# Attention scores of four heads on 32 rows each with three half-precision products, six score banks and half-bank projections

## The chip, the cores and the metric

The kernel runs on one core of one Trainium2 chip. The metric is the device time of one execution in microseconds (us); the time of a kernel is the median of several runs. The core has TensorE (PE, matrix multiplication into PSUM), VectorE (DVE), ScalarE (ACT), GpSimd (POOL) and SyncE (SP, here the queue that issues most transfers). PSUM has eight banks, each of 512 single-precision columns on 128 partitions.

## The reference

The input is one sequence of 2048 positions with 1024 features. Two layers follow each other, and each has an attention block and a spectral block (a two-dimensional Fourier filter). The change is in the attention block.

```python
def _A_ref(x, wqkv, wo):
    B, S, D = x.shape                      # 1, 2048, 1024
    H = 32
    Dh = D // H                            # 32
    qkv = (x @ wqkv).reshape(B, S, 3, H, Dh).transpose(2, 0, 3, 1, 4)
    q, k, v = qkv[0], qkv[1], qkv[2]
    scores = jnp.einsum("bhqd,bhkd->bhqk", q, k) * (Dh ** -0.5)
    p = _softmax(scores, axis=-1)
    o = jnp.einsum("bhqk,bhkd->bhqd", p, v)
    return o.transpose(0, 2, 1, 3).reshape(B, S, D) @ wo

x = A_x
x = x + _A_ref(_layernorm(x), A_wqkv, A_wo)
x = x + _B_ref(_layernorm(x), B_w_r, B_w_i)
x = x + _A_ref(_layernorm(x), A_wqkv, A_wo)
x = x + _B_ref(_layernorm(x), B_w_r, B_w_i)
```

## The kernel before

The 32 heads are worked in eight groups `g` of four heads. A group has four chunks `c` of 512 queries and sixteen key tiles `kt` of 128 keys. Everything is transposed: the features lie on partitions, and a score tile has keys on partitions and queries along the free dimension.

Projections work on values that `split` has cut into a high and a low float16 half (ScalarE writes the high half, L160, VectorE the rest, L161). `qk_chunk` makes 512 positions of the queries or keys of a group: eight feature blocks by three products (high by high, high by low, low by high) accumulate in one PSUM bank (L305), then `split` reads the bank into `hl`. `v_tile` does the same for 128 positions of the values of two groups, 256 columns wide (L372), and ScalarE alone reads the bank (L376).

The queries and keys of four heads come out one below the other, 32 features each. They are stored to a DRAM tile `db` (L315) and loaded again (`spread`, L329) so that each head's tile has four blocks of 32 rows: for the keys high, high, low, low, and for the queries high, low, high, low. One matmul over 128 rows therefore gives the sum of all four products of the halves for one head (`S`, L551). Two heads share a PSUM tile `s` of two banks, and ScalarE takes the exponential of the 1024 columns (L553) into `p`, in single precision. The bias of the exponential is a bound worked out from the norms of queries and keys (`norms`, `mkbias`).

`PV` (L561) multiplies `p` by the values: four heads, each 32 output columns, write the four quarters of the partitions of one bank `o`, over the sixteen key tiles. VectorE adds the tiles of `p` up (L564, L566) into `acc` for the denominators. After the last key tile `fin` sums `acc` over partitions with ones (L571, in an `x` bank), and VectorE transposes, inverts and multiplies (L573 to L579).

The order of instructions on TensorE is the order of the program. For each key tile it issues the scores of two heads, some steps of a filler, the scores of the other two heads, more of the filler. At even key tiles it issues the value matmuls of the two earlier key tiles. The filler is the projections of the groups to come, and in the last group and the end of the one before, the output projection (`wo_part` without the last group of heads, `wo_tile` with it, L438), whose result VectorE adds to the residual (L452, L466).

PSUM holds two score tiles of two banks each, two `o` banks, and two `x` banks that serve the projections, the norms, the denominators and the output projection in turn:

```python
    psS = psum("at_psS", 2, space=PSUM)
    psO = psum("at_psO", 2, space=PSUM)
    psX = psum("at_psX", 2, space=PSUM)
```

Of the kernel before, what the change touches and what calls it, by code (L numbers as in the profile page):

```python
# [100 lines left out]
SX = 2.0 ** 8  # L101
# [5 lines left out]
WO_STEPS = 12 * 48  # L107
# [74 lines left out]
class AttnPools:  # L182


    def __init__(self, tc):
        self.tc = tc
        self.low = Pools(tc, "left")
        self.big = self.low("at_x", 1).tile([128, 16384], F32, name="big")
        self.right = Pools(tc, "right")
        r = self.right("at_r", 1).tile([128, 16384], F32, name="R")  # L190
        self.x = r.rearrange("p (t d) -> p t d", d=1024)
        k = r.bitcast(F16).rearrange("p (t h n) -> p t h n", h=4, n=2048)
        self.k = [k[:, i] for i in (1, 2)]
# [10 lines left out]
    def open_small(self):  # L204
        small = self.small = Pools(self.tc, "left")
        self.pp = small("at_p", 7)
        self.qp = small("at_q", 2)
        self.hl = small("at_hl", 2)
# [46 lines left out]
SPILL = [2, 3, 8, 9, 10, 11]  # L255
# [3 lines left out]
def attention(nc, tc, layer, ap, xin, yd, xnd, wts, wo, cst, dram, flags):  # L259
# [5 lines left out]
    pp, qp, hl, sgp, wqp, wvp = ap.pp, ap.qp, ap.hl, ap.sgp, ap.wqp, ap.wvp  # L265
    sq, on, on2, sm = ap.sq, ap.on, ap.on2, ap.sm
    db = psum("at_db", 20, space=DRAM)
# [5 lines left out]
    V, K, Q, kd, qd, bias, nrm, mx = {}, {}, {}, {}, {}, {}, {}, {}  # L273
    cur = [0]
# [24 lines left out]
    def qk_chunk(ph, c):  # L299
        kind, g = ph  # L300
        w = W[ph]
        ps = psX.tile([128, 512], F32, name="x")
        for d in range(8):
            for i, (a, b) in enumerate(((w[:, 0, d], xh[c][:, d]), (w[:, 0, d], xl[c][:, d]), (w[:, 1, d], xh[c][:, d]))):
                nc.tensor.matmul(ps, a, b, start=d == 0 and i == 0, stop=d == 7 and i == 2)  # L305
                if d < 7 or i < 2:
                    yield
        t = hl.tile([128, 2, 512], F16, name="hl")
        split(nc, t[:, 0], t[:, 1], ps, SQ / (SX * SW))
        if c == 0:  # L310
            p_, n_ = (qp, "Q") if ph == ("q", 0) else (sq, "sq")
            nrm[ph] = p_.tile([128, 4, 512], BF16, name="sq", tag=n_)
        nc.gpsimd.tensor_tensor(nrm[ph][:, c], t[:, 0], t[:, 0], op=ALU.mult)  # L313
        d_ = db.tile([2, 128, 512], F16, name="db")
        nc.sync.dma_start(d_.rearrange("a p n -> p a n"), t)  # L315
        if kind == "k":
            if c == 0:
                K[g] = ap.k[g % 2]
            kd[g, c] = d_
            if g <= cur[0] + 1:  # L320
                load_k(g)
        else:
            qd[g, c] = d_
        yield

    def spread(dst, d_, parts):

        for j, a in enumerate(parts):
            nc.sync.dma_start(dst[32 * j:32 * j + 32], d_[a].rearrange("(h p) n -> p h n", p=32))  # L329

    def load_k(g):
        for c in range(NCH):
            if (g, c) in kd:
                spread(K[g][:, :, c * 512:(c + 1) * 512], kd.pop((g, c)), (0, 0, 1, 1))

    def load_q(g, c):
        Q[g, c] = qp.tile([128, 4, 512], F16, name="Q")
        spread(Q[g, c], qd.pop((g, c)), (0, 1, 0, 1))

    def norms(ph):  # L340
        kind, g = ph
        if g not in mx:
            mx[g] = sm.tile([128, 2], F32, name="mqk")
        ps = psX.tile([128, 512], F32, name="x")
        for c in range(4):
            nc.tensor.matmul(ps[32 * c:32 * c + 32], cst["bones"], nrm[ph][:, c], start=True, stop=True)
        i = 0 if kind == "k" else 1
        nc.vector.reduce_max(mx[g][:, i:i + 1], ps, axis=AX.X)
        if kind == "q":
            mkbias(g)  # L350
        yield

    def mkbias(g):
        r = sm.tile([128, 2], F32, name="mall")
        nc.gpsimd.partition_all_reduce(r, mx[g], 128, bass.bass_isa.ReduceOp.max)
        b = sm.tile([128, 1], F32, name="bpr")
        nc.gpsimd.tensor_tensor(b, r[:, 0:1], r[:, 1:2], op=ALU.mult)
# [4 lines left out]
    def v_tile(ph, t):  # L362
# [5 lines left out]
        ps = psX.tile([128, 512], F32, name="x")  # L368
        for d in range(8):
            a, b = xh[c][:, d, o:o + 128], xl[c][:, d, o:o + 128]  # L370
            for i, (l, r) in enumerate(((a, w[:, 0, d]), (a, w[:, 1, d]), (b, w[:, 0, d]))):
                nc.tensor.matmul(ps[:, :256], l, r, start=d == 0 and i == 0, stop=d == 7 and i == 2)  # L372
                if (3 * d + i) % 2 and d * 3 + i < 23:
                    yield
# [12 lines left out]
    def filler():  # L387
        run(prep(phases[0]))
        for i, ph in enumerate(phases):
# [12 lines left out]
            for n, _ in enumerate(body()):  # L402
                if n % 16 == 12:
                    next(nxt, None)
                yield
# [23 lines left out]
    def wo_mm(c, t, n, ds):  # L429

        p = psX.tile([128, 512], F32, name="x")
        last = 3 * len(ds) - 1
        k = 0
        for d in ds:
            oh, ol = ((olast[c][:, i] if d == 7 else osb[c][:, i, d])[:, t * 128:t * 128 + 128] for i in range(2))
            wh, wl = (wo_t[i][d // 4][:, d % 4, n * 512:n * 512 + 512] for i in range(2))
            for a, b in ((oh, wh), (oh, wl), (ol, wh)):
                nc.tensor.matmul(p, a, b, start=k == 0, stop=k == last)  # L438
                k += 1
                if k <= last:  # L440
                    yield
        return p

    def wo_part(c, t, dst):
# [4 lines left out]
        for n in range(2):  # L449
            p = yield from wo_mm(c, t, n, range(7))  # L450
            sl = slice(n * 512, n * 512 + 512)
# [3 lines left out]
    def wo_tile(c, t, dst, part=False):  # L455
# [6 lines left out]
        for n in range(2):  # L462
            p = yield from wo_mm(c, t, n, (7,) if part else range(8))
            sl = slice(n * 512, n * 512 + 512)
            src = dst if part else x
            nc.vector.scalar_tensor_tensor(x[:, sl], p, 1.0 / (SO * SW), src[:, sl], op0=ALU.mult, op1=ALU.add)  # L466
            nc.vector.bn_stats(st[:, n], x[:, sl])
            if not part:
                fold(nc, x, dst, slice(4 * n, 4 * n + 4))
            if n:  # L470
# [8 lines left out]
    def wo_filler():  # L479
# [10 lines left out]
        while rests:  # L490
# [3 lines left out]
            elif parts and (parts[0] < 11 or pos[0] > 98):  # L494
# [4 lines left out]
                if t == 10:  # L499
                    dst[t] = sq.tile([128, 1024], F32, name="sq")  # L500
                if t == 11:
                    dst[t] = qp.tile([128, 1024], F32, name="Q")
# [3 lines left out]
            else:  # L506
                yield True
# [32 lines left out]
    load_q(0, 0)  # L540
# [6 lines left out]
    def S(g, c, kt, hf):  # L547
        s = psS.tile([128, 2, 512], F32, name="s")
        for j in range(2):
            h = hf * 2 + j  # L550
            nc.tensor.matmul(s[:, j], K[g][:, h, kt * 128:(kt + 1) * 128], Q[g, c][:, h], start=True, stop=True)  # L551
        p = P[g, c, kt, hf] = pp.tile([128, 2, 512], F32, name="p")
        nc.scalar.activation(p, s, AF.Exp, bias=bias[g], scale=SCALE / (SQ * SQ))  # L553

    def PV(g, c, kt, hf):
        if kt == 0 and hf == 0:
            O[g, c] = psO.tile([128, 512], F32, name="o")
        p = P[g, c, kt, hf]
        for j in range(2):
            h = hf * 2 + j  # L560
            nc.tensor.matmul(O[g, c][32 * h:32 * h + 32], V[g][:, kt, 32 * h:32 * h + 32], p[:, j],  # L561
                             start=kt == 0, stop=kt == NKT - 1)
        if kt == 1:
            nc.vector.scalar_tensor_tensor(acc[hf], P[g, c, 0, hf], 1e-34, p, op0=ALU.add, op1=ALU.add)  # L564
        elif kt:
            nc.vector.tensor_add(acc[hf], acc[hf], p)  # L566

    def fin(g, c):
        z = psX.tile([128, 512], F32, name="x")
        for h in range(4):  # L570
            nc.tensor.matmul(z[32 * h:32 * h + 32], cst["ones"], acc[h // 2][:, h % 2], start=True, stop=True)  # L571
        zt = on.tile([128, 16, 32], F32, name="zt")
        nc.vector.transpose(zt.rearrange("p a b -> p (a b)"), z)  # L573
# [14 lines left out]
    pend = []  # L588
    fill, lwo, wof = filler(), load_wo(), wo_filler()
    left, n_wo, go = 16, 0, 0  # L590
    with tc.manual_schedule(engines={mybir.EngineType.PE}):
        for g in range(NG):
            cur[0] = g
            total = sum(steps(ph) for ph in beside.get(g, []))
            got = 0
            for u in range(NCH * NKT):
                c, kt = divmod(u, NKT)
                for hf in range(2):
                    S(g, c, kt, hf)
                    i = 2 * u + hf + 1  # L600
                    pos[0] = i if g == NG - 1 else 0
                    if i == 4 and (g + 1, 0) in kd:
                        load_k(g + 1)
                    nq = (g, c + 1) if c + 1 < NCH else (g + 1, 0)
                    if i % 32 > 2 and nq in qd:
                        load_q(*nq)
                    while got < min(total, total * i / (126 if g < NG - 2 else 112)):
                        next(fill, None)
# [4 lines left out]
                    if g == NG - 1 or (g == NG - 2 and got == total and not left):  # L613
                        go += (WO_STEPS - n_wo) / (129 - i + 128 * (NG - 1 - g))
                        while n_wo + 1 <= go:
                            if next(wof, None):
# [3 lines left out]
                    pend.append((g, c, kt, hf))  # L620
                    while hf and kt % 2 == 0 and len(pend) > 2:
                        w = pend.pop(0)
                        PV(*w)
                        if w[2] == NKT - 1 and w[3] == 1:
                            fin(w[0], w[1])
            if (g + 1, 0) in qd:
                load_q(g + 1, 0)
            if g == NG - 2:
                run(lwo)
        for w in pend:  # L630
# [4 lines left out]
    for i, t, n in ((0, 2, 2), (2, 8, 4)):  # L635
# [19 lines left out]
def spectral(nc, tc, ap, yd, xout, a, cst, fast, flags=None, nxt=None):  # L655
# [221 lines left out]
    def ai(i, tt):  # L877
# [6 lines left out]
        if i % 2 == 0:  # L884
            sd[0] = ap.qp.tile([128, 8, 128], F32, name="sd0", tag="Q")
            sd[1] = ap.pp.tile([128, 8, 128], F32, name="sd1", tag="p")
# [247 lines left out]
```

## Time and profile before

| | |
|---|---|
| median of 3 runs | 4070.28 us (4067.77 to 4073.4) |
| the profiled execution | 4067.89 us, span of the core 4066.1 us, granted TensorE clock 0.99 |
| TensorE busy | 3883.5 us, 96% of the span |
| VectorE busy | 3279.8 us, 81% |
| ScalarE busy | 2823.8 us, 69% |
| GpSimd busy | 711.7 us, 18% |
| attention loop, layer 1 | first score matmul at 123.4 us |
| attention loops, end | last score matmul of layer 2 at 3745.0 us |

A line of a group in the page has the line of the kernel, the engine, the operation, what it writes and reads, shapes and count; behind the bar the busy time in us and the mean in ns of one instruction; behind the second bar the time in which the engine had been idle just before such an instruction, and what ended it. Matmuls are pipelined, so the mean of one (379 ns) is longer than the time by which it advances the engine. PEld is the loading of the weights, which overlaps matmuls. In a timeline the two first columns are the start and the time covered by the merged instructions, both in us.

### The profile page before, as it was taken

The page shows a single profiled execution, that of the slowest core. Times are in us where ns is not written, and L with a number is a line of the kernel's source. Part 1 is how long each engine was busy: PE and PEld are TensorE (multiplying, and loading weights), DVE is VectorE, ACT ScalarE, POOL GpSimd, SP SyncE. Part 2 cuts the span into 40 slices and gives each one's busy share as a digit, 9 for nine tenths or more (in the row PEclk, how much of TensorE's full clock was granted, in tenths as well). Part 3 has the DMA queues.
Part 4 walks back from the last instruction along what each step waited for, and adds up shares of the span by engine and source line. Part 5 has one row for each costly group of instructions (what it writes and reads, how often), then busy time and mean ns, then how long its engine had stood idle before and what let it go on. Part 6 is the DMA issues. An engine that isn't in the chain of part 4 may idle for free.

```text
span 4066.1 us, 65193 instructions
## 1 busy us (share of the span) xinstructions
PE 3883.5 (96%) x25012; PEld 1843.3 (45%) x25012; DVE 3279.8 (81%) x4059; ACT 2823.8 (69%) x3597; POOL 711.7 (18%) x625
## 2 busy tenths in 40 slices
PE   8899999999999999999888999999999999999998
PEld 5333533443344333378853335334433443333797
DVE  6698889889988988956755987888888889889456
ACT  4577777777777865548645777777777778655485
POOL 1111011101210112314311110111011101122143
PEclk9999999999999999999989999999999999999999
DMA  4221022102200323253132210221022003232433
GB/s 149 66 63 53 17 60 64 44 19 68 65 30 24 97 71 103 89 204 96 52 120 66 63 53 17 63 66 39 19 71 63 29 24 101 71 100 90 157 109 99
DMA packets 209378, 289.64 MB, mean 71 GB/s; under 512 B 17696, under 2 KB 161696, under 8 KB 208032
## 3 DMA queue, kind: packets, MB, share of 16 engines
q1 hardware_dynamic: 207312, 279.03, 21.5%
q10 hardware_dynamic: 1744, 6.36, 0.4%
q8 instruction: 198, 3.24, 0.3%
q14 instruction: 124, 1.02, 0.1%
HBM read 197.23 MB, written 88.08 MB: 70 GB/s over the span
## 4 chain that ended last, share of the span: by engine, by line
PE 74%; issue 8%; DVE 8%; ACT 4%; POOL 3%; DMA 2%; ACTq 0%; DVEq 0%; POOLq 0%; SPq 0%
PE o L561 20%; PE s L551 19%; PE x L305 13%; PE x L372 7%; PE x L438 5%; ACT p L553 3%; DVE R L566 2%; PE ps L767 2%; PE ps L705 1%; PE x L571 1%; DMA w<-in_w 1%; POOL sq L313 1%; PE ps L696 1%; PE ps L882 1%; PE ps L870 1%
## 5 line engine op out<-in xcount | busy, mean ns | idle before, releaser
L553 ACT ACTIVATE p<-s,bias 128x1024 f32<-128x1024 f32 x2048 | 2168.0, 1117 | 851.3 <-PE s L551 816.8
L566 DVE TENSOR_TENSOR R<-R,p 128x1024 f32<-128x1024 f32 x1792 | 2189.9, 1273 | 237.7 <-ACT p L553 233.0
L551 PE MATMUL s<-Q,R 128*128 128x512 f16 x4096 | 1219.9, 380 | 49.9 <-ACT p L553 47.9
L561 PE MATMUL o<-p,R 128*32 128x512 f32 x8192 | 991.4, 600 | 0.0
L305 PE MATMUL x<-big,wqk 128*128 128x512 f16 x3072 | 858.8, 379 | 2.3 <-DVE hl L161 2.3
L551 PEld LDWEIGHTS <-R 128*128 128x128 f16 x4096 | 357.4, 97 | 811.8 <-issue 559.0
L305 PEld LDWEIGHTS <-wqk 128*128 128x128 f16 x3072 | 299.9, 98 | 365.1 <-issue 6.8
L561 PEld LDWEIGHTS o<-p,R 128*32 128x32 f32 x8192 | 218.1, 109 | 513.0 <-issue 508.1
L372 PE MATMUL x<-wv,big 128*128 128x256 f16 x3072 | 425.5, 274 | 15.3 <-DVE hl L161 5.9
L313 POOL TENSOR_TENSOR sq<-hl 128x512 bf16<-128x512 f16 x128 | 200.5, 1567 | 1191.4 <-ACT hl L160 1191.0
L372 PEld LDWEIGHTS <-big 128*128 128x128 f16 x3072 | 300.7, 98 | 161.6 <-DVE big L161 6.8
L438 PE MATMUL x<-big 128*128 128x512 f16 x1344 | 334.8, 379 | 3.8 <-DVE xres L466 2.8
L582 POOL TENSOR_TENSOR ohl<-zt,ohl 128x512 f16<-128x512 f32 x64 | 102.6, 1602 | 1221.4 <-ACT ohl L581 1179.1
L438 PEld LDWEIGHTS <-big 128*128 128x128 f16 x1344 | 131.1, 98 | 164.7 <-issue 6.2
L564 DVE SCALAR_TENSOR_TENSOR R<-p 128x1024 f32<-128x1024 f32 x128 | 153.2, 1197 | 26.8 <-ACT p L553 26.8
L573 DVE STREAM_TRANSPOSE zt<-x 128x512 f32<-128x512 f32 x64 | 45.9, 717 | 124.9 <-PE x L571 124.6
L161 DVE SCALAR_TENSOR_TENSOR hl<-x,hl 128x512 f16<-128x512 f32 x128 | 87.2, 681 | 59.1 <-ACT hl L160 55.5
L815 DVE TENSOR_TENSOR H<-G,H 128x512 f16<-128x512 f32 (+1 forms) x68 | 46.5, 683 | 105.4 <-ACT H L814 105.3
L160 ACT ACTIVATE hl<-x 128x512 f16<-128x512 f32 x128 | 77.2, 603 | 56.5 <-issue 41.9
L760 ACT COPY U<-ps 64x256 f32<-64x256 f32 (+1 forms) x272 | 97.2, 357 | 7.9 <-PE ps L767 2.9
L767 PE MATMUL ps<-cbi,H 128*128 128x256 f16 (+1 forms) x792 | 99.0, 273 | 3.8 <-ACT H L814 1.8
L760 ACT COPY B<-ps 64x256 f32<-64x256 f32 (+1 forms) x272 | 97.1, 357 | 6.7 <-PE ps L767 2.4
(408 smaller groups left out, 2990.7 us busy)
## 6 DMA issues: line engine op xcount, KB each, us to landing
db<-hl SPq DMA_DIRECT2D x128, 256.0 KB, 2.2
R<-db SPq DMA_DIRECT2D x256, 128.0 KB, 2.8
Q<-db SPq DMA_DIRECT2D x256, 128.0 KB, 2.8
wst<-in_wp SPq DMA_DIRECT2D x96, 256.0 KB, 3.1
y<-xres SPq DMA_DIRECT2D x32, 512.0 KB, 2.9
R<-y SPq DMA_DIRECT2D x32, 512.0 KB, 5.1
w<-in_w SPq DMA_DIRECT2D x60, 256.0 KB, 2.7
od<-ohl SPq DMA_DIRECT2D x56, 256.0 KB, 2.3
```

The lines of the kernel that those rows point to most:

```text
L305: nc.tensor.matmul(ps, a, b, start=d == 0 and i == 0, stop=d == 7 and i == 2)
L313: nc.gpsimd.tensor_tensor(nrm[ph][:, c], t[:, 0], t[:, 0], op=ALU.mult)
L372: nc.tensor.matmul(ps[:, :256], l, r, start=d == 0 and i == 0, stop=d == 7 and i == 2)
L438: nc.tensor.matmul(p, a, b, start=k == 0, stop=k == last)
L551: nc.tensor.matmul(s[:, j], K[g][:, h, kt * 128:(kt + 1) * 128], Q[g, c][:, h], start=True, stop=True)
L553: nc.scalar.activation(p, s, AF.Exp, bias=bias[g], scale=SCALE / (SQ * SQ))
L561: nc.tensor.matmul(O[g, c][32 * h:32 * h + 32], V[g][:, kt, 32 * h:32 * h + 32], p[:, j], start=kt == 0, stop=kt == NKT - 1)
L564: nc.vector.scalar_tensor_tensor(acc[hf], P[g, c, 0, hf], 1e-34, p, op0=ALU.add, op1=ALU.add)
L566: nc.vector.tensor_add(acc[hf], acc[hf], p)
L582: nc.gpsimd.tensor_tensor(t[:, 1], r, t[:, 0], op=ALU.subtract)
L760: nc.scalar.copy(ov[64 * r:64 * r + 64, a0:a0 + m, x], tl[64 * x:64 * x + 64, :m, r])
L767: nc.tensor.matmul(out, l, r, start=k == 0, stop=k == len(mm_) - 1)
```

## The change

- The keys and queries stay in the chip's memory as a high and a low half, with the heads on their own 32 rows. `qk_chunk` writes them there directly, and the DRAM copies and `spread` are gone. A score is now three products (high by high, high by low, low by high), each a matmul over 32 rows; the four heads' matmuls stand next to each other and write four different banks.
- Score tiles: three of two banks instead of two. `o` has one bank instead of two; ScalarE copies it out after the last key tile of a chunk. The `x` bank is one instead of two: a tile `xb` of two halves of 256 columns, which the users take in turn.
- Projections, output projection, norms and denominators work on 256 columns at a time. A step of the filler is two matmuls of 256 columns.
- The filler is issued at odd key tiles only, all of a pair's steps in one block after the scores. Before `fin` the filler runs on until no accumulation is open in `xb` (`boundary`). `fin` of a chunk comes one pair of key tiles later.
- Smaller ones: eight `p` buffers instead of seven; two fewer output tiles pass through DRAM (`SPILL`); the steps of the output projection are 52 instead of 48 a tile; the spectral block takes two buffers from another pool.

```diff
-    psS = psum("at_psS", 2, space=PSUM)
-    psO = psum("at_psO", 2, space=PSUM)
-    psX = psum("at_psX", 2, space=PSUM)
+    psS = psum("at_psS", 3, space=PSUM)
+    psO = psum("at_psO", 1, space=PSUM)
+    xb = psum("at_psX", 1, space=PSUM).tile([128, 2, 256], F32, name="x")
+    xi = itertools.count()
+    def psX():
+        return xb[:, next(xi) % 2]
...
-        ps = psX.tile([128, 512], F32, name="x")
-        for d in range(8):
...
-        split(nc, t[:, 0], t[:, 1], ps, SQ / (SX * SW))
...
-        nc.sync.dma_start(d_.rearrange("a p n -> p a n"), t)
...
+        t = (K if kind == "k" else Q)[g]
+        for o in range(c * 512, c * 512 + 512, 256):
+            ps = psX()
+            x = slice(o % 512, o % 512 + 256)
+            for d in range(8):
+                h, l = xh[c][:, d, x], xl[c][:, d, x]
+                for i, (a, b) in enumerate(((w[:, 0, d], h), (w[:, 0, d], l), (w[:, 1, d], h))):
+                    nc.tensor.matmul(ps, a, b, start=d == 0 and i == 0, stop=d == 7 and i == 2)
+                    if (3 * d + i) % 2 and d * 3 + i < 23:
+                        yield OPEN
+            split(nc, t[:, 0, o:o + 256], t[:, 1, o:o + 256], ps, SQ / (SX * SW))
...
-    def S(g, c, kt, hf):
-        s = psS.tile([128, 2, 512], F32, name="s")
-        for j in range(2):
-            h = hf * 2 + j
-            nc.tensor.matmul(s[:, j], K[g][:, h, kt * 128:(kt + 1) * 128], Q[g, c][:, h], start=True, stop=True)
-        p = P[g, c, kt, hf] = pp.tile([128, 2, 512], F32, name="p")
-        nc.scalar.activation(p, s, AF.Exp, bias=bias[g], scale=SCALE / (SQ * SQ))
+    def S(g, c, kt):
+        s = [psS.tile([128, 2, 512], F32, name="s") for _ in range(2)]
+        for i, (a, b) in enumerate(((0, 0), (0, 1), (1, 0))):
+            for h in range(4):
+                r = slice(32 * h, 32 * h + 32)
+                nc.tensor.matmul(s[h // 2][:, h % 2], K[g][r, a, kt * 128:kt * 128 + 128],
+                                 Q[g][r, b, c * 512:c * 512 + 512], start=i == 0, stop=i == 2)
+        for hf in range(2):
+            p = P[g, c, kt, hf] = pp.tile([128, 2, 512], F32, name="p")
+            nc.scalar.activation(p, s[hf], AF.Exp, bias=bias[g], scale=SCALE / (SQ * SQ))
...
+        if kt == NKT - 1:
+            o = ap.oc.tile([128, 512], F32, name="oc")
+            nc.scalar.copy(o, O[g, c])
+            O[g, c] = o
...
+        for n in range(2):
+            z = psX()
+            for h in range(4):
+                nc.tensor.matmul(z[32 * h:32 * h + 32], cst["ones"], acc[h // 2][:, h % 2, 256 * n:256 * n + 256], start=True, stop=True)
+            nc.vector.transpose(zt[:, 8 * n:8 * n + 8].rearrange("p a b -> p (a b)"), z)
...
+    def boundary(f):
+        n = 0
+        while last[0] == OPEN:
+            step(f)
+            n += 1
+        return n
...
+                S(g, c, kt)
+                if kt % 2 == 0:
+                    for w in pend:
+                        PV(*w)
+                        if done:
+                            fin(*done.pop())
+                    done = [w[:2] for w in pend if w[2] == NKT - 1]
+                    pend = []
+                pend.append((g, c, kt))
...
+                    while kt % 2 and got < min(total, total * i / (126 if g < NG - 2 else 112)):
+                        step(fill)
                         got += 1
...
+                if done and kt % 2:
+                    if n_wo:
+                        n_wo += boundary(wof)
+                    else:
+                        got += boundary(fill)
```

More of the change, by code (lines that the diff above doesn't have):

```diff
@@ L301, in qk_chunk @@
         w = W[ph]
-        ps = psX.tile([128, 512], F32, name="x")
-        for d in range(8):
[L304 to L308, printed above, removed]
-        split(nc, t[:, 0], t[:, 1], ps, SQ / (SX * SW))
         if c == 0:
+            if kind == "k":
+                K[g] = ap.k[g % 3]
+            else:
+                Q[g] = qp.tile([128, 2, 2048], F16, name="Q") if g % 2 else ap.q
@@ L324, in qk_chunk @@
[L324 to L338, printed above, removed]
+        t = (K if kind == "k" else Q)[g]
@@ L342, in norms @@
         if g not in mx:
[L343 to L348, printed above, removed]
+            mx[g] = sm.tile([128, 2, 2], F32, name="mqk")
+        for n in range(2):
+            ps = psX()
+            for c in range(4):
+                nc.tensor.matmul(ps[32 * c:32 * c + 32], cst["bones"], nrm[ph][:, c, 256 * n:256 * n + 256], start=True, stop=True)
+            i = 0 if kind == "k" else 1
+            nc.vector.reduce_max(mx[g][:, i, n:n + 1], ps, axis=AX.X)
         if kind == "q":
@@ L429, in wo_mm @@
     def wo_mm(c, t, n, ds):
-        p = psX.tile([128, 512], F32, name="x")
+        p = psX()
         last = 3 * len(ds) - 1
@@ L439, in wo_mm @@
                 k += 1
-                if k <= last:
-                    yield
+                if k <= last and k % 2 == 0:
+                    yield OPEN
         return p
@@ L461, in wo_tile @@
         st = sm.tile([128, 2, 6], F32, name="st")
-        for n in range(2):
+        for n in range(4):
             p = yield from wo_mm(c, t, n, (7,) if part else range(8))
-            sl = slice(n * 512, n * 512 + 512)
+            sl = slice(n * 256, n * 256 + 256)
             src = dst if part else x
             nc.vector.scalar_tensor_tensor(x[:, sl], p, 1.0 / (SO * SW), src[:, sl], op0=ALU.mult, op1=ALU.add)
[L467 to L470, printed above, removed]
+            if n % 2:
+                nc.vector.bn_stats(st[:, n // 2], x[:, (n - 1) * 256:(n + 1) * 256])
+                if not part:
+                    fold(nc, x, dst, slice(2 * n - 2, 2 * n + 2))
+            if n == 3:
                 if part:
@@ L568, in fin @@
     def fin(g, c):
-        z = psX.tile([128, 512], F32, name="x")
-        for h in range(4):
-            nc.tensor.matmul(z[32 * h:32 * h + 32], cst["ones"], acc[h // 2][:, h % 2], start=True, stop=True)
         zt = on.tile([128, 16, 32], F32, name="zt")
-        nc.vector.transpose(zt.rearrange("p a b -> p (a b)"), z)
+        for n in range(2):
+            z = psX()
+            for h in range(4):
+                nc.tensor.matmul(z[32 * h:32 * h + 32], cst["ones"], acc[h // 2][:, h % 2, 256 * n:256 * n + 256], start=True, stop=True)
+            nc.vector.transpose(zt[:, 8 * n:8 * n + 8].rearrange("p a b -> p (a b)"), z)
@@ L586, in fin, with step @@
             olast[c] = t
-    pend = []
+    pend, done, last = [], [], [None]
+    def step(f):
+        last[0] = next(f, None)
+        return last[0]
+    def boundary(f):
[4 more added lines that the diff above has]
+        return n
     fill, lwo, wof = filler(), load_wo(), wo_filler()
@@ L597, in attention @@
                 c, kt = divmod(u, NKT)
-                for hf in range(2):
-                    S(g, c, kt, hf)
-                    i = 2 * u + hf + 1
-                    pos[0] = i if g == NG - 1 else 0
[L602 to L608, printed above, removed]
+                S(g, c, kt)
[7 more added lines that the diff above has]
+                pend.append((g, c, kt))
+                for i in (2 * u + 1, 2 * u + 2):
+                    pos[0] = i if g == NG - 1 else 0
+                    while kt % 2 and got < min(total, total * i / (126 if g < NG - 2 else 112)):
+                        step(fill)
                         got += 1
@@ L614, in attention @@
                         go += (WO_STEPS - n_wo) / (129 - i + 128 * (NG - 1 - g))
-                        while n_wo + 1 <= go:
-                            if next(wof, None):
+                        while kt % 2 and n_wo + 1 <= go:
+                            if step(wof) == IDLE:
                                 go = n_wo
@@ L884, in ai @@
         if i % 2 == 0:
-            sd[0] = ap.qp.tile([128, 8, 128], F32, name="sd0", tag="Q")
-            sd[1] = ap.pp.tile([128, 8, 128], F32, name="sd1", tag="p")
+            for g in range(2):
+                sd[g] = ap.pp.tile([128, 8, 128], F32, name="sd", tag="p")
         e = ap.on.tile([128, 4, 128], F32, name="e", tag="zt")
```

105 lines of the change are left out of this document (46 added, 59 removed).

## The prediction

> **What bounds the kernel now.** I read the page first: the share of each engine, then the costliest groups.
>
> ```profile
> PE 3883.5 (96%) x25012; PEld 1843.3 (45%) x25012; DVE 3279.8 (81%) x4059; ACT 2823.8 (69%) x3597; POOL 711.7 (18%) x625
> ...
> L553 ACT ACTIVATE p<-s,bias 128x1024 f32<-128x1024 f32 x2048 | 2168.0, 1117 | 851.3 <-PE s L551 816.8
> L566 DVE TENSOR_TENSOR R<-R,p 128x1024 f32<-128x1024 f32 x1792 | 2189.9, 1273 | 237.7 <-ACT p L553 233.0
> L551 PE MATMUL s<-Q,R 128*128 128x512 f16 x4096 | 1219.9, 380 | 49.9 <-ACT p L553 47.9
> L561 PE MATMUL o<-p,R 128*32 128x512 f32 x8192 | 991.4, 600 | 0.0
> L305 PE MATMUL x<-big,wqk 128*128 128x512 f16 x3072 | 858.8, 379 | 2.3 <-DVE hl L161 2.3
> ...
> L161 DVE SCALAR_TENSOR_TENSOR hl<-x,hl 128x512 f16<-128x512 f32 x128 | 87.2, 681 | 59.1 <-ACT hl L160 55.5
> ...
> L160 ACT ACTIVATE hl<-x 128x512 f16<-128x512 f32 x128 | 77.2, 603 | 56.5 <-issue 41.9
> ```
>
> TensorE is busy 96% of the span; ScalarE waits for its scores (816.8 us) and VectorE for ScalarE. TensorE waited for almost nothing: 47.9 us for a score buffer and, over 3072 projection matmuls, 2.3 us for a projection bank to be read out. Next I read the busy time by stretch: the steady loop of each layer, a stretch with value projections, and the output projection.
>
> ```profile
> 1000.00:1100.00 100.00, 96.16 (x564) 33.65 (x561) 90.46 (x96) 75.29 (x80) 20.84 (x12) 1.00 0.22 63
> ...
> 1200.00:1300.00 100.00, 98.74 (x698) 46.01 (x697) 81.42 (x75) 75.56 (x94) 3.79 (x2) 1.00 0.06 17
> ...
> 1600.00:1700.00 100.00, 95.27 (x533) 35.17 (x532) 94.71 (x146) 58.35 (x54) 32.72 (x22) 1.00 0.24 85
> ```
>
> The columns are PE, PEld, DVE, ACT, POOL. TensorE is the bound throughout; VectorE is 17 points behind it with the value projections, 6 with queries and keys, and level with it in the output projection. Last the timeline of one pair of key tiles, which is the unit of the loop (256 pairs in a layer, 512 in all).
>
> ```profile
> 302.47 0.81 PE L305 MATMUL x<-big,wqk 128*128 128x512 f16 x3
> 303.21 0.16 PEld L561 LDWEIGHTS o<-p,R 128*32 128x32 f32 x8 [0.42 <-issue]
> 303.21 1.92 PE L561 MATMUL o<-p,R 128*32 128x512 f32 x16
> 303.67 0.13 PEld L561 LDWEIGHTS o<-p,R 128*32 128x32 f32 x4 [0.30 <-issue]
> 303.87 0.62 ACT L160 ACTIVATE hl<-x 128x512 f16<-128x512 f32 x1
> 304.10 0.13 PEld L561 LDWEIGHTS o<-p,R 128*32 128x32 f32 x4 [0.30 <-issue]
> ...
> 305.07 0.61 PE L551 MATMUL s<-Q,R 128*128 128x512 f16 x2
> 305.51 0.59 PE L305 MATMUL x<-big,wqk 128*128 128x512 f16 x2
> 305.57 0.68 DVE L161 SCALAR_TENSOR_TENSOR hl<-x,hl 128x512 f16<-128x512 f32 x1
> 305.95 0.59 PE L551 MATMUL s<-Q,R 128*128 128x512 f16 x2
> 306.38 0.59 PE L305 MATMUL x<-big,wqk 128*128 128x512 f16 x2
> 306.88 0.59 PE L551 MATMUL s<-Q,R 128*128 128x512 f16 x2
> 307.31 0.81 PE L305 MATMUL x<-big,wqk 128*128 128x512 f16 x3
> 307.96 0.59 PE L551 MATMUL s<-Q,R 128*128 128x512 f16 x2
> 308.39 0.59 PE L305 MATMUL x<-big,wqk 128*128 128x512 f16 x2
> 308.91 1.92 PE L561 MATMUL o<-p,R 128*32 128x512 f32 x16
> ```
>
> One matmul of 512 columns advances TensorE by (0.81 - 0.379)/2 = 0.216 us. The sixteen value matmuls, on 32 columns each, go four side by side: the weight loads of a four are 0.43 us apart, so 4 x 0.43 = 1.72 us, but the block holds TensorE 305.07 - 303.21 = 1.86 us. From 305.07 to 308.91 stand 8 score and 9 projection matmuls, 17 x 0.216 = 3.67 of 3.84 us. So a change of the array's tiling costs about 0.15 us each way, twice a pair now.
>
> **Scores.** A key tile costs 4 matmuls over 128 rows now, 0.86 us, and becomes 12 over 32 rows: three rounds of four heads. If four row strips run side by side as the four column strips of the value matmuls do, that is 3 x 0.216 = 0.65 us; if they do not, 12 x 0.216 = 2.59 us. I take 0.65, because the nearest row (eight column-strip loads in 0.16 us, four matmuls per 0.43 us) shows strips loading and running together. A pair saves 2 x 0.216 = 0.43 us. But the order becomes scores, values, scores, projections: four changes of tiling instead of two, +0.30 us. Net -0.13 us, x512 = -67 us.
>
> The Trainium skill, "TensorE: Matmul & The Clock Gate", section "Measured speedup vs the span model", speaks against even this: four row tiles of 512 columns measured 3.07 times, not 4. By it the twelve cost an estimated 2.59/3.07 = 0.84 us, as much as now, and the sum would be about 200 us higher; no row here shows row strips, so the trace can neither agree nor differ.
>
> **Projections, the term that decides.** Before, a group of 24 matmuls filled one of two x banks, and the next group started in the other while ScalarE (L160) and VectorE (L161) read the first out. The diff leaves one bank, `xb`, whose halves the groups take in turn. No row of before shows TensorE writing a bank while another engine reads a different part of it, so the price has two ends: 0 if halves are independent, and the whole read-out if TensorE must wait for it. I take the whole wait: both halves are one tile in one bank, and the diff itself closes an open group before the denominators touch the other half, so they are not treated as separate buffers.
>
> The rule for it is in the Trainium skill, "PSUM — Partial Sum Buffer", section "PSUM bank collisions raise a hardware error": TensorE and a reader must be kept apart by bank and 32-partition quadrant, whatever the address. By that rule the two halves give no double buffering; the trace has no case that tests it.
>
> How long a read-out takes is in the trace. Above, the group ends at 302.47 + 0.81 = 303.28 and L161 at 305.57 + 0.68 = 306.25: 2.97 us, most of it VectorE's queue of additions. Two others:
>
> ```profile
> 977.38 0.81 PE L305 MATMUL x<-big,wqk 128*128 128x512 f16 x3
> ...
> 979.49 0.68 DVE L161 SCALAR_TENSOR_TENSOR hl<-x,hl 128x512 f16<-128x512 f32 x1
> ...
> 1007.53 0.81 PE L305 MATMUL x<-big,wqk 128*128 128x512 f16 x3
> ...
> 1011.97 0.68 DVE L161 SCALAR_TENSOR_TENSOR hl<-x,hl 128x512 f16<-128x512 f32 x1
> ```
>
> These are 980.17 - 978.19 = 1.98 and 1012.65 - 1008.34 = 4.31 us; the mean of three is 3.09. Half the width saves about 0.26 us on each engine, from (1117 - 603)/512 = 1.0 ns per element on ScalarE: 2.57. As TensorE stalls, VectorE's queue shortens, so I take 2.3 us (ends 1.5 and 3.8). The projections now come in one block per pair, about 9.6 steps of two matmuls of 256 columns; a group is 12 steps, so nine of ten group ends fall inside a block and the next step stalls at once.
>
> - Query and key groups: 14 phases x 4 chunks x 2 halves x 2 layers = 224, x0.9 x2.3 = 464 us.
>
> ```profile
> L376 ACT ACTIVATE R<-x x256: 254/279/307, 24.0 to 3310.0; 128x128 f32<-128x128 f32 x128
> L573 DVE STREAM_TRANSPOSE zt<-x x64: 706/717/718, 184.3 to 3752.7; 128x512 f32<-128x512 f32 x64
> L452 DVE SCALAR_TENSOR_TENSOR R<-x,xres x32: 674/683/692, 1457.3 to 3645.8; 128x512 f32<-128x512 f32 x32
> ```
>
> - Value groups in the loop: 3 x 16 x 2 = 96. ScalarE alone reads them: it starts 303.87 - 303.28 = 0.59 us late, then 2 x 0.279: about 1.25 us with the hand-over. 96 x 0.9 x 1.25 = 108 us.
> - Output projection: 12 tiles x 4 widths x 2 (part and rest) x 2 layers = 192 groups, read by VectorE: half an addition ahead of it (0.64), 0.683 - 0.26 = 0.42, and about 0.15 of hand-over: 1.2 us. 230 us. These stall at every group, since a rest is 3 matmuls.
> - Norms: 28 x 2 halves x 1.2 = 67 us. Denominators: the second half waits for the first transpose, 0.717 - 0.26 + 0.3 = 0.8 us, x64 = 51 us; it now comes a pair later, when the additions are done.
> - Before and after the loops, the first projections and the last output tiles lose the second bank too: some 64 groups and 32 groups at 0.6 to 1.1 us, part of it behind transposes and normalisation: 60 us.
>
> **What costs nothing.** The DMAs of queries and keys through DRAM go (128 stores at L315, 512 loads at L329) with their SP issues; they were hidden: the first exponentials wait for the bias, as the last fence shows. The copy of O on ScalarE (64 x about 0.62 us) and the third score buffer lie on ScalarE, which has 25% free; if its slack went, it would delay the read-outs priced above. VectorE gets about 0.15 us more for each split halved: 25 us a layer, off the path as long as TensorE stalls. With one O bank the first value matmul of the next chunk waits for that copy, issued a pair before it. Halving the projection width costs TensorE nothing in columns.
>
> Sum: 464 + 108 + 230 + 67 + 51 + 60 - 67 = +913 us on the profiled execution's 4067.9 us (span 4066.1), 4981; that execution is 2.4 us under the median of the runs shown, so about 4980 us against 4070.3.
>
> **The rivals.**
> *Halves independent: faster.* If TensorE may write one half during the read-out of the other, all the stalls fall away, and 4070 - 67 = about 4005 us remains, plus some of VectorE's 50 us where it is already 95% busy: 3990 to 4060. For it: two halves would be pointless otherwise. Against: one tile, one bank. It decides where a read-out costs TensorE less than 67/700, or 0.1 us a group. Chance 0.14.
> *Row strips or their weights do not overlap.* With 0.097 us for each of twelve loads in turn, a key tile takes 1.16 us instead of 0.65: +0.51 x 1024 = +525 us, 5500 us with the stalls. For: twelve loads and twelve matmuls in 0.65 us is a denser issue than any row shows. Against: the column strips. A partial overlap, at 0.2 us a key tile between the 0.65 and the 1.16, gives +205 us, 5185, and is counted here. 0.12.
> *Short read-outs.* With TensorE stalled, VectorE and ScalarE have little queued and each read-out is near its own 0.35 + 0.42 us: the 913 halves, about 4400 to 4500 us. 0.14.
>
> **How the numbers follow.** The main case has 0.60 and gives 4980; its own range, with 1.5 to 3.8 us for a read-out (-160, +300), the other groups scaled alike and some row loss, is 4600 to 5400. Two more things push up: TensorE's clock,
>
> ```profile
> 2167.98 3.33 ACT L553 ACTIVATE p<-s,bias 128x1024 f32<-128x1024 f32 x3 [10.65 <-POOL bias L360]
> ...
> 2169.95 1.49 PE L305 MATMUL x<-big,wqk 128*128 128x512 f16 x3
> ...
> 2173.30 0.81 PE L305 MATMUL x<-big,wqk 128*128 128x512 f16 x3
> ```
>
> which after that wait ran at half rate (1.49 against 0.81 us for three), and could fall again if stalls run together. To hold 8 in 10 I take in the short read-outs and the row rival up to 5500, and leave out the faster case: 4090 to 5500. Faster by over 0.2% (what can be told from no change here): 0.14; within: 0.02; slower: 0.84.
>
> **What would show it.** After the change the groups at the projection matmuls should show idle time of several hundred us before them, released by the reads of the hi and lo halves, of V and of the residual; TensorE's share near 80%. If instead they show a few us, the first rival holds. The score matmuls should come twelve in about 0.65 us plus a fill; 1.2 us or more means the second. I am wrong above all if the halves turn out to be two buffers.

## The result: 36% slower, and the profile after

The changed kernel takes 5554.4 us (median of 4 runs, 5551.9 to 5557.4) against 4069.5 us: a ratio of 1.365, interval 1.362 to 1.367. The forecast was 4980 us with a range of 4090 to 5500, so the direction was right, and the size was 54 us above the top of the range.

These are the lines of the page of the changed kernel that answer to those of before: the engines' busy time, the granted clock in 40 slices (9 is full), and the groups.

```profile
PE 4304.2 (77%) x38452; PEld 2257.9 (41%) x38452; DVE 3325.0 (60%) x4411; ACT 2886.3 (52%) x3789; POOL 639.8 (12%) x625
...
PEclk9888988898889888889997889888988898988899
...
L549 ACT ACTIVATE p<-s,bias 128x1024 f32<-128x1024 f32 x2048 | 2164.2, 1112 | 1893.3 <-PE s L545 1837.0
L562 DVE TENSOR_TENSOR R<-R,p 128x1024 f32<-128x1024 f32 x1792 | 2181.2, 1260 | 959.9 <-ACT p L549 959.3
L321 PE MATMUL x<-big,wqk 128*128 128x256 f16 x6144 | 889.6, 303 | 534.5 <-DVE R L162 361.3
L555 PE MATMUL o<-p,R 128*32 128x512 f32 x8192 | 1121.4, 664 | 0.0
...
L545 PE MATMUL s<-R 32*128 32x512 f16 x6144 | 508.0, 423 | 67.1 <-ACT p L549 67.0
L545 PE MATMUL s<-Q,R 32*128 32x512 f16 x6144 | 472.3, 407 | 37.4 <-ACT p L549 37.4
L366 PE MATMUL x<-wv,big 128*128 128x256 f16 x3072 | 404.5, 286 | 119.7 <-ACT R L370 107.8
```

Two things stand in them. The projections, before which TensorE had waited 2.3 us, now have 534.5 us of idle time in front. And the busy time of TensorE rose too, by 4304.2 - 3883.5 = 421 us, though by the prediction's sum its work shrank by 67 us; the value matmuls, which the change leaves as they were, went from 991 to 1121 us. The span grew by 5555.0 - 4066.1 = 1489 us: 421 us busy and 1068 us idle (1250.8 against 182.6).

What TensorE waited for, in us in total, times, and the longest:

```profile
PE x L321 <- DVE R L162: 361.3, 130, 6.0
PE x L321 <- DVE Q L162: 157.9, 46, 6.4
PE x L366 <- ACT R L370: 107.8, 85, 2.2
PE s L545 <- ACT p L549: 104.4, 78, 11.0
PE x L432 <- DVE R L446: 89.7, 68, 2.6
PE x L432 <- DVE xres L460: 84.5, 116, 2.0
PE x L337 <- DVE mqk L339: 54.6, 34, 4.9
PE x L337 <- DVE R L162: 42.0, 8, 5.9
PE x L573 <- DVE zt L574: 39.6, 61, 1.7
PE x L337 <- DVE Q L162: 26.9, 8, 4.6
...
PE x L432 <- DVE wv L446: 16.8, 14, 2.7
```

One such wait in the timeline of the changed kernel, and what comes behind it:

```profile
225.43 1.05 PE L321 MATMUL x<-big,wqk 128*128 128x256 f16 x8
225.53 2.12 ACT L549 ACTIVATE p<-s,bias 128x1024 f32<-128x1024 f32 x2 [0.89 <-PE s L545]
226.68 2.36 DVE L562 TENSOR_TENSOR R<-R,p 128x1024 f32<-128x1024 f32 x2 [0.64 <-ACT p L549]
227.54 0.38 ACT L161 ACTIVATE R<-x 128x256 f16<-128x256 f32 x1
...
228.96 0.42 DVE L162 SCALAR_TENSOR_TENSOR R<-x,R 128x256 f16<-128x256 f32 x1
229.43 1.69 PE L321 MATMUL x<-big,wqk 128*128 128x256 f16 x10 [2.95 <-DVE R L162]
231.05 1.47 PE L545 MATMUL s<-R 32*128 32x512 f16 x12
...
234.80 0.83 PE L545 MATMUL s<-R 32*128 32x512 f16 x12
```

A group ends at 226.48. ScalarE reads it only after its two exponentials, VectorE after two additions, and at 229.43 the next group starts in the other half: 2.95 us of nothing. The ten projection matmuls and twelve score matmuls behind the wait then run slowly, 1.47 us for what takes 0.83 us a few us later. That is the granted clock: it is full or half in the records (half here from 230.09 to 233.50 us), so a mean of 0.884 means 2 x 0.116 x 5555 = about 1289 us at half clock (the records add up to 1286); before it was 79.

### The profile page after: what moved, and what is told of

The parts are those of the page before. It is cut to its first block, busy times and chain, and to the rows that moved or that the text cites. A ratio compares the mean times of both kernels' runs of the same rounds, so it can differ in the third digit from the quotient of the medians.

```text
span 5555.0 us, 91491 instructions
## 1 busy us (share of the span) xinstructions
PE 4304.2 (77%) x38452; PEld 2257.9 (41%) x38452; DVE 3325.0 (60%) x4411; ACT 2886.3 (52%) x3789; POOL 639.8 (12%) x625
## 4 chain that ended last, share of the span: by engine, by line
PE 53%; DVE 18%; issue 17%; ACT 8%; POOL 2%; DMA 2%; DVEq 0%; ACTq 0%; POOLq 0%; SPq 0%
PE o L555 14%; PE s L545 12%; PE x L321 10%; DVE R L562 6%; ACT p L549 6%; PE x L366 5%; PE x L432 5%; DVE R L560 2%; PE x L573 1%; PE ps L718 1%; DVE R L162 1%; PE ps L780 1%; DVE zt L574 1%; DMA wst<-in_wp 1%; DMA w<-in_w 1%
## 5 line engine op out<-in xcount | busy, mean ns | idle before, releaser
L321 PE MATMUL x<-big,wqk 128*128 128x256 f16 x6144 | 889.6, 303 | 534.5 <-DVE R L162 361.3
L555 PE MATMUL o<-p,R 128*32 128x512 f32 x8192 | 1121.4, 664 | 0.0
L321 PEld LDWEIGHTS <-wqk 128*128 128x128 f16 x6144 | 634.9, 107 | 815.2 <-issue 694.0
L545 PEld LDWEIGHTS <-R 32*128 32x128 f16 x12288 | 248.7, 97 | 870.9 <-issue 774.9
L545 PE MATMUL s<-R 32*128 32x512 f16 x6144 | 508.0, 423 | 67.1 <-ACT p L549 67.0
L545 PE MATMUL s<-Q,R 32*128 32x512 f16 x6144 | 472.3, 407 | 37.4 <-ACT p L549 37.4
L366 PE MATMUL x<-wv,big 128*128 128x256 f16 x3072 | 404.5, 286 | 119.7 <-ACT R L370 107.8
L432 PE MATMUL x<-big 128*128 128x256 f16 x2688 | 344.1, 284 | 123.2 <-DVE R L446 73.2
L366 PEld LDWEIGHTS <-big 128*128 128x128 f16 x3072 | 302.4, 102 | 238.5 <-issue 190.4
L432 PEld LDWEIGHTS <-big 128*128 128x128 f16 x2688 | 267.6, 101 | 208.6 <-issue 170.0
L327 POOL TENSOR_TENSOR sq<-R 128x512 bf16<-128x512 f16 x96 | 148.3, 1545 | 1363.4 <-ACT R L161 1363.4
L432 PE MATMUL x<-big,ohl 128*128 128x256 f16 x384 | 83.8, 338 | 114.7 <-DVE xres L460 57.0
L337 PE MATMUL x<-sq,bones 128*32 128x256 bf16 x256 | 27.2, 353 | 126.2 <-DVE mqk L339 54.6
```

The costliest lines, as they stand in the source:

```text
L327: nc.gpsimd.tensor_tensor(nrm[ph][:, c], h, h, op=ALU.mult)
L366: nc.tensor.matmul(ps, l, r, start=d == 0 and i == 0, stop=d == 7 and i == 2)
L545: nc.tensor.matmul(s[h // 2][:, h % 2], K[g][r, a, kt * 128:kt * 128 + 128], Q[g][r, b, c * 512:c * 512 + 512], start=i == 0, stop=i == 2)
```

## The experiments

Each time is of one run; the kernel before took 4069 to 4071 us beside them.

**Is it the bank?** The two halves are given two banks, still in one tile. Four score banks make room.

```diff
-    psS = psum("at_psS", 3, space=PSUM)
+    psS = psum("at_psS", 2, space=PSUM)
-    xb = psum("at_psX", 1, space=PSUM).tile([128, 2, 256], F32, name="x")
+    xb = psum("at_psX", 1, space=PSUM).tile([128, 2, 512], F32, name="x")
-        return xb[:, next(xi) % 2]
+        return xb[:, next(xi) % 2, 0:256]
```

> Two changes to the kernel after: the two x halves lie in two different banks (256 columns used of each), and the score tiles go back from three to two to make room. Theory A (the time goes to TensorE waiting for the read-out of the shared x bank, and the low clock is a consequence of these waits): idle before the projection matmuls falls from 534 us to under 60 us, half-clock time from 1286 us to under 300 us, and a new wait of 200 to 450 us appears before the score matmuls, because a key tile now needs both score tiles free; time 4350 to 4650 us. Theory B (32-row matmuls themselves pull the clock down): the x waits go too, but the granted clock stays near 0.88 and the time is 4800 us or more. Theory C (the halves were independent all along and the waits are VectorE being late): the x waits stay above 300 us.

The control has the first of these edits alone:

```diff
-    psS = psum("at_psS", 3, space=PSUM)
+    psS = psum("at_psS", 2, space=PSUM)
```

> The control for the run with two x banks: only the score tiles go back from three to two, the x halves stay in one bank. Theory A: the x waits stay (450 to 550 us before the projection matmuls), some score waits are added, the time is 5500 to 5850 us. If instead the time falls by more than 300 us, the third score tile and not the x bank is to blame.

Measured: 5636.1 us with two banks, 5617.6 us with one. The first line is from the page of the two banks, the second from the control's.

```profile
L321 PE MATMUL x<-big,wqk 128*128 128x256 f16 x6144 | 880.5, 301 | 446.1 <-DVE R L162 304.6
```

```profile
L321 PE MATMUL x<-big,wqk 128*128 128x256 f16 x6144 | 878.9, 301 | 442.6 <-DVE R L162 300.6
```

A second bank changed nothing: A, which had put the wait down to the bank, and B, by which these waits would have gone as well, both failed here. C's number came (446 us, above 300), but not yet its reason. The control held its time, with 443 us of waits just under its range. What the two halves still had in common is the tile, so they were made two tiles:

```diff
-    xb = psum("at_psX", 1, space=PSUM).tile([128, 2, 256], F32, name="x")
+    xp = psum("at_psX", 2, space=PSUM)
+    xb = [xp.tile([128, 512], F32, name="x") for _ in range(2)]
-        return xb[:, next(xi) % 2]
+        return xb[next(xi) % 2][:, 0:256]
```

(with four score banks again)

> As the run with two x banks, but the banks are two separate tiles and not two parts of one tile; four score banks. That run showed that a second bank within one tile leaves the waits as they are. Theory D (the order is kept by the tile: a matmul into any part waits for all readers of the tile, whatever the bank): idle before the projection matmuls falls from 446 to under 60 us, the clock to 0.96 or above, and waits for the two score tiles bind instead; time 4300 to 4650 us. Theory E (something else holds the next group, for instance the weights or the halves written): waits above 300 us and 5500 us or more as before.

Measured: 4576.6 us, granted clock 0.950. The first line is from its page, the second from its waits.

```profile
L322 PE MATMUL x<-big,wqk 128*128 128x256 f16 x6144 | 761.8, 281 | 16.0 <-DVE mqk L340 15.9
```

```profile
PE s L546 <- ACT p L550: 218.8, 223, 9.8
```

Same columns, same count of banks, same order as in the run at 5636 us: 446 us of waiting became 16, and 1060 us of time went. The order is kept for the whole tile, and C's reason falls too: VectorE's read-out is no faster here (0.42 us), but the next group no longer waits for it. The clock came out a little under the 0.96 expected, with waits for the two score tiles in place of the others.

**What lowers the clock?** Two causes were possible: the waits, or the 32-row matmuls. First, useless matmuls go into the waits of the changed kernel.

```diff
+    def warm(n):
+        if fresh[0] or cur[0] is None:
+            return
+        if ahead[0] is None:
+            ahead[0] = psS.tile([128, 2, 512], F32, name="s")
+        k = K[cur[0]]
+        for j in range(n):
+            nc.tensor.matmul(ahead[0][:, j % 2], k[:, 0, 0:128], k[:, 0, 0:512], start=True, stop=True)
...
+            warm(12)
             ps = psX()
```

> The kernel after with useless matmuls of 512 columns put ahead of each group that would start right behind another in the same block of projections: 12 for queries and keys (2.6 us), 5 for values, 4 for the output projection; they write a score tile that the next scores overwrite. They fall into the time in which TensorE waits for the x bank. Theory A with the clock as a consequence of the waits: the half-clock time falls from 1286 us to under 400 us and the time falls to 5000 to 5250 us, although some 2000 matmuls are added. Theory B (32-row matmuls pull the clock down): clock unchanged, time 5550 us or more.

Measured: 5347.6 us, granted clock 0.956; 469 us at half clock instead of 1286. From its page:

```profile
PE 4648.9 (87%) x41514; PEld 2478.2 (46%) x41514; DVE 3320.7 (62%) x4411; ACT 2881.7 (54%) x3789; POOL 649.3 (12%) x625
...
L340 PE MATMUL s<-R 128*128 128x512 f16 x3062 | 755.4, 389 | 0.0
```

The kernel got 207 us faster by 3062 matmuls of no use. Without them TensorE's busy time is 4648.9 - 755.4 = 3893.5 us, 411 us less than in the changed kernel and 10 more than before. The low clock costs at least that, since 469 us at half clock are left (under 400 were expected). The time fell less than the 300 to 550 us expected, because the fill was in places longer than the wait it replaced: idle time fell by 1250.8 - 696.8 = 554 us for 755 us of fill. Half the fill, at queries and keys alone:

```diff
-            warm(12)
+            warm(6)
...
-        warm(5)
...
-        warm(4)
```

> The run with filled waits, with half the fill: 6 useless matmuls (1.3 us) ahead of a query or key group that starts right behind another, none at the values and the output projection. If the clock drops only after a window of 3.41 us in which TensorE was idle for more than about 1.9 us (in the runs so far no such window was followed by full clock), a query or key wait of some 3 us is cut to under that limit, so half the fill does most of the work: half-clock time between 470 and 700 us (469 with the full fill, 1286 with none), time 5300 to 5420 us. If the clock follows the idle time in proportion, half the fill gives about half the gain: half-clock time about 900 us, time 5430 to 5480 us.

Measured: 5418.3 us, 855 us at half clock. Neither forecast came whole: the half-clock time is near the proportional one (900 us), well above the limit's 470 to 700 us, while the time lies just inside the limit's 5300 to 5420 us and 12 us under the other's. Its waits before queries and keys were still

```profile
PE x L322 <- DVE R L162: 217.0, 118, 4.7
PE x L322 <- DVE Q L162: 105.2, 40, 5.0
```

322 us of 519, so many stayed long. The expectation from a limit, that half the fill does most of the work, failed. That does not refute a limit: of 213 gaps of 2 us or more on TensorE, 144 were left, and the section on the hardware has what the records say.

Second, waits without 32-row matmuls: the kernel before with one full x bank for the projections.

```diff
-    psX = psum("at_psX", 2, space=PSUM)
+    psX = psum("at_psX", 1, space=PSUM)
+    psZ = psum("at_psZ", 1, space=PSUM)
...
-        z = psX.tile([128, 512], F32, name="x")
+        z = psZ.tile([128, 512], F32, name="x")
```

(and the same for the bank of `norms`)

> The kernel before with one x bank of full width for the projections instead of two; the other bank is kept for norms and denominators alone. No 32-row matmul, the order of the filler unchanged. Theory A (waits for the read-out pull the clock down): idle before the projection and output matmuls rises from about 25 to 400 to 600 us, half-clock time rises from 79 to 300 us or more, time 4650 to 5000 us. Theory B (the 32-row matmuls pull it down): the waits come, but the clock stays at 0.97 or above and the time is 4450 to 4650 us, that is 4070 and the waits alone.

Measured: 4714.7 us, granted clock 0.957, 412 us at half clock. Its page and its waits:

```profile
PE 4072.5 (86%) x25012; PEld 1868.3 (40%) x25012; DVE 3284.6 (70%) x4059; ACT 2839.7 (60%) x3597; POOL 677.2 (14%) x625
```

```profile
PE x L306 <- DVE hl L161: 251.7, 85, 4.5
PE x L373 <- ACT R L377: 106.0, 97, 1.5
PE x L439 <- DVE xres L467: 61.5, 56, 2.9
```

The span grew by 647 us: 458 idle and 189 busy. The waits alone lower the clock, with the old scores and the old order. This is also the projection bank's part of the change done alone, in a milder form: the filler stands between the scores there, and the groups of queries, keys and the output projection are half as many.

**Does the order of the filler matter?** Each block of projections is one whole group, so that the read-out has nearly a pair of key tiles to finish in.

```diff
-                    while kt % 2 and got < min(total, total * i / (126 if g < NG - 2 else 112)):
-                        step(fill)
-                        got += 1
+                    if kt % 2 and i % 2 == 0 and got < min(total, total * i / (126 if g < NG - 2 else 112)):
+                        while step(fill) == OPEN:
+                            pass
+                        got += 1
```

(`total` counts groups, and `norms` is cut in two)

> The kernel after with another order of the filler alone: each block of projections is one whole group of 24 matmuls, so the read-out has the next scores and values of a whole pair of key tiles to finish in; the norms are cut into their two halves, a block each. The output projection keeps its order. Theory A: idle before the projection matmuls of queries, keys and values falls from 654 us to under 80 us, half-clock time to under 500 us, time 4350 to 4650 us, with the output projection's waits (some 230 us) left. Theory B: the clock stays near 0.88 and the time is above 4800 us.

Measured: 4620.2 us, granted clock 0.954. One pair of key tiles on TensorE in its timeline, and the two largest of its waits:

```profile
1002.97 0.83 PE L545 MATMUL s<-R 32*128 32x512 f16 x12
1003.72 1.92 PE L555 MATMUL o<-p,R 128*32 128x512 f32 x16
1005.58 0.82 PE L545 MATMUL s<-R 32*128 32x512 f16 x12
1006.45 2.78 PE L321 MATMUL x<-big,wqk 128*128 128x256 f16 x24
1009.16 0.82 PE L545 MATMUL s<-R 32*128 32x512 f16 x12
```

```profile
PE s L545 <- ACT p L549: 226.3, 178, 10.6
PE x L432 <- DVE R L446: 88.1, 68, 3.4
```

With half banks, one tile and 32-row scores all kept, the order took 934 us back, and half-clock time fell to 430 us, as theory A had it. Then the output projection was put into whole groups too, at three places of a pair, with other banks for the first and last tiles:

```diff
+        if where[0] == "tail":
+            return psS.tile([128, 2, 512], F32, name="s")[:, 0, 0:256]
+        n = next(xi) % 2
+        if where[0] == "head" and n:
+            return psO.tile([128, 512], F32, name="o")[:, 0:256]
...
-                        while kt % 2 and n_wo + 1 <= go:
+                        if i % 2 == 0:
+                            n_wo, go = whole(n_wo, go)
```

> The kernel after with whole groups per block for the queries, keys and values as before, and now for the output projection too: at most three groups in a pair of key tiles, at three places with scores or values between them. The first projections alternate between the x bank and the idle o bank, and the last output tiles use the idle score banks. Theory A: the waits before the output projection fall from some 220 to under 100 us and the half-clock time from 430 to under 250 us; time 4200 to 4400 us. It stays above the kernel before, because the scores save only 67 us by the sum. If the time does not fall below 4500, the output projection's loss of about 110 us a layer has another cause than these waits.

Measured: 4435.2 us, 333 us at half clock, both above what was expected (up to 4400, under 250). It is still 366 us slower than before: its span is 367 us longer, 311 idle (494.0 against 182.6) and 56 busy. Its page and its waits:

```profile
PE 3939.4 (89%) x38452; PEld 2184.3 (49%) x38452; DVE 3309.8 (75%) x4411; ACT 2897.3 (65%) x3789; POOL 710.8 (16%) x625
```

```profile
PE s L551 <- ACT p L555: 229.2, 193, 10.0
PE x L438 <- DVE xres L466: 45.1, 18, 4.0
```

The largest is now TensorE waiting for a score tile (47.9 us before). Where a pair has no group, TensorE has less to do (about 0.76 + 1.86 + 0.76 = 3.4 us for scores and values) than ScalarE (four exponentials of 1.11 us), and the three score tiles do not let it run ahead. That this makes up the rest is read from the waits, not tested.

## Why the prediction was right in direction and too low

**The waits: nearly right in total, with errors that partly offset.** By the waits of the changed kernel, queries and keys cost 361.3 + 157.9 = 519 us (forecast 464), values 107.8 (108), the output projection's read-outs by VectorE 89.7 + 84.5 + 16.8 = 191 (230), norms 54.6 + 42.0 + 26.9 = 124 (67), denominators 40 (51). With the smaller ones the idle time rose by 1068 us against 980 forecast. The norms were under-sized: 54.6 us are waits for a reduction on VectorE, up to 4.9 us at a time, and 42.0 + 26.9 us waits for the split of the last query or key group.

**The step that failed is the sum's omission of the clock.** The prediction quoted the rows that show it, matmuls at half rate after a wait, and named it as something that "push[es] up", but gave it no term. Filling the waits took 411 us of its cost back and left 469 us at half clock. The traces give an estimate of the whole: TensorE was busy for 960 of the 1286 us at half clock, and at full clock the same work would take half as long, so the price is about 480 us; before, it was 37 / 2 = 19. The missing term is thus about 461 us. Of the 5556.8 - 4981 = 576 us that the sum missed, the remaining 115 are 1068 - 980 = 88 us of idle time and some 27 us of the saving that did not come.

**The saving of 67 us.** The price of the scores was right. In the pair of the run with whole groups above, scores hold TensorE for 1003.72 - 1002.97 = 0.75 and 1006.45 - 1005.58 = 0.87 us with the change of tiling (the median over that run's full-clock stretches is 0.76 ahead of values and ahead of projections alike), twelve 32-row matmuls against 2.59 us one after another; the pair takes 6.19 us with 24 projection matmuls, and the old order needs 1.73 + 1.72 + 2.59 + 0.30 = 6.34. So the four row strips do run together, and the second rival, at 1.16 us, is refuted. The Trainium skill's 3.07 times ("TensorE: Matmul & The Clock Gate", "Measured speedup vs the span model") would have been an estimated 0.84 us; the median here is 0.76 with the switch, 3.4 times. The busy time without the low clock's estimated price is 4304.2 - 480 = 3824 us against 3883.5 - 19 = 3865 before, so some 41 of the 67 us were saved on TensorE. But no run without the long waits came near 4005 us: in the best, at 4435.2 us, idle time was 311 us longer, most of it in waits for score tiles (229.2 us against 47.9).

**The reason for the waits was half right.** I gave "one tile in one bank", and the Trainium skill's rule by bank ("PSUM — Partial Sum Buffer", "PSUM bank collisions raise a hardware error") beside it. The runs show the tile: two banks in one tile wait as one bank does (446 and 443 us), two tiles do not (16 us). Whether accesses to one bank through two tiles would be ordered too was not tried. The first rival asked whether halves are independent; they are not, and two banks of one tile are not either.

**The third rival** (short read-outs, half the loss) is refuted: at queries and keys the wait is (361.3 + 157.9)/(130 + 46) = 2.95 us in the mean, about as long as a read-out before the change (3.09). In the timeline of the wait above, two exponentials on ScalarE and two additions on VectorE stand ahead of the read-out. The sum had 2.3 us for about 202 such waits; they were longer and fewer, 176.

## What to carry to other kernels

In these runs a slice of a tile is no buffer: what one engine may write while another reads was decided by the tile, so buffers that take turns need tiles of their own, or an order that leaves the read-out enough other work. Price a wait on TensorE twice: its own length, and the matmuls behind it at half clock; here 1068 us of idle time brought an estimated 461 us of low clock. When a change trades one resource for several (six score banks for the second x bank), cost the one that is given up first: its reader's queue was 3 us long in the trace, against 0.13 us saved a pair.

## What the runs showed of the hardware

The granted clock changes in steps of 3.413 us. The Trainium skill, "TensorE: Matmul & The Clock Gate", section "What's actually happening", has that window and half clock after an idle one; the records agree on the window, but a window need not be idle throughout. In all ten kernels, with the matmul rows laid beside the clock records, no window that was followed by full clock had more than 2.04 us without a matmul, and the window just ahead of a fall to half clock had 1.44 us at the least, with medians from 2.2 to 2.6 us by kernel; between 1.44 and 2.04 us either came. So waits well under 3.4 us are enough.

The count of long gaps tells more than the idle time. In the changed kernel, with half the fill and with the full fill, TensorE had 213, 144 and 79 gaps of 2 us or more, 230, 146 and 81 stretches at half clock, and 1286, 855 and 469 us in them, while idle time was 1251, 1049 and 697 us. Shorter gaps count too when they fall into one window: with two tiles, 84 stretches came with only 44 such gaps.
